# Weight decoding moved partly into the first stage, and filter products in batches of four pairs, in a long-convolution kernel with two MoE layers

## The chip, the cores and the metric

The kernel runs on one core of one Trainium2 chip. The metric is the device time of one execution in microseconds (us). An execution profiled by the hardware gives the trace; the time of that execution stands beside its span.

## The reference, cut to what matters

The sequence has S = 12480 rows of D = 128. First a gated long convolution, then two feed-forward layers with 2048 hidden units:

```python
h_filt = (np.maximum(pos_emb @ w1, 0.0) @ w2) * window        # window = exp(-0.01 * pos)
u = x * v
y = irfft(rfft(u, 2 * S) * rfft(h_filt, 2 * S), 2 * S)[:S]
x = x * y
x = np.maximum(x @ w_in, 0.0) ** 2 @ w_out                    # moe
g = elu(x @ w_in2);  out = g @ w_out2                         # moe2
```

All weights of the two layers reach the kernel as 64-bit floats (each pair of 32-bit words is one number).

## The kernel before, in words

The transform length is L = 181 * 127, and the convolution is done by matrices in three stages. **Stage 1** (`phase1`, lines 179 to 305) folds x * v and the filter's hidden layer and transforms over 181 points: 16 groups of eight channels in a loop over j, each with two calls of `s1` (line 276, 16 matmuls each, line 281), 32 calls in all; the index of the call is i. `prologue(i)` (line 347) hangs other work onto that loop: at i = 15 the loads of the filter's last matrix, of the matrix g and of the first six tables `tb` (line 310); at i = 24 `s2r(0)`; at i = 31 `hmm(0)`. The x tiles of stage 1 live in ten rotating buffers `xc` of the pool `xv`.

**Stage 2** (`phase2`, line 439) goes over NP = 46 pairs of frequencies, p = 0 to 45. Pair p needs on TensorE `s2(p)` (line 461, tile u, the transform of x * v), every second pair `s2r(q)` (line 321, tile rt, the filter's transform of two pairs at once, copied by ScalarE to `rr`) and, one pair later, `hmm(q)` (line 332, tile h: 16 matmuls with 64 rows each, copied by ScalarE to `hh`). VectorE multiplies (`prod`, lines 478 and 479), GpSimd adds and subtracts (lines 481 and 482), TensorE transforms back (`ia`, line 489, tile v, two pairs later), ScalarE copies to z, and SyncE stores z to a buffer in HBM (line 495, and line 500 for the first rows of the last pairs).

Between these, `weights` (line 419) is a generator that decodes and splits the 16 chunks of weights. It is advanced four times per pair; a place, in what follows, is such a step. A chunk's `decode` (line 373) takes four VectorE instructions (lines 380, 382, 391, 393), three of ScalarE (385, 387, 389) and one product on GpSimd (399). Its `split` (line 403) takes a ScalarE copy and a GpSimd subtraction (line 131). A chunk is begun every WDEC = 10 steps, at most WF = 5 are decoded ahead of the splits, and the splits of chunks 0 to 3, 4 to 7 and 8 to 15 wait for pairs 8, 16 and 32 (line 430). Loading (`load_weights`, line 362) runs two chunks ahead in two buffers `raw`.

Each engine works in program order. The order of the work is the order of the calls in the loop at line 554. PSUM has eight banks: in stage 2 two hold u, two v, two h (one buffer, `hbank`) and two rt (two buffers). The pool `p2b` of stage 2 lies where `xv` was, and its first use waits for the last use of `xv`.

**Stage 3** (`phase3`, line 607) runs both layers over 26 tiles of columns. `head` (line 515) prepares its first tile in stage 2.

```python
        while ns < 16 or gs is not None:
            if gd is None and nd < 16 and nd - ns < WF and i >= WDEC * nd:
                gd, nd = self.decode(nd), nd + 1
```

Of the kernel before, what the change touches and what calls it, by code (L numbers as in the profile page):

```python
# [10 lines left out]
F32 = mybir.dt.float32  # L11
F32R = mybir.dt.float32r
U32 = mybir.dt.uint32
AF = mybir.ActivationFunctionType
ALU = mybir.AluOpType
SYNC = mybir.DependencyInfo(mybir.DependencyClass.Sync, mybir.DependencyReason.DATA)
PSUM = bass.MemoryType.PSUM
# [3 lines left out]
D = 128  # L21
# [3 lines left out]
N2 = 127  # L25
# [4 lines left out]
NP = (K1 + 1) // 2  # L30
R = 99
SPLIT = S - (R - 1) * N2
SIZES = (4,) + 24 * (5,) + (3,)
KTAIL = K1 - 64
TBB = 6
WF = 5
AGE = 4
PD = NP - 2
PZ = PD - 4
HD = (33, 35, 36, 37, 38, PZ + 2)  # L40
KD = K1 - 2 * PD
WDEC = 10
OFF = 3
LAG1 = 2
NX = 10
# [75 lines left out]
class Build:  # L121
# [52 lines left out]
        return self.psb[0].tile([128, 2, 512], F32, tag="h", name="h")  # L174

    def rbank(self):
        return self.psb[1].tile([128, 512], F32, tag="rt", name="rt") if len(self.psb) > 1 else self.hbank()[:, 0]

    def phase1(self):
        nc, a = self.nc, self.a  # L180
        with ExitStack() as ctx1:
# [5 lines left out]
            ns = [0]  # L187
# [15 lines left out]
            xvp = self.right.enter_context(self.tc.tile_pool(name="xv", bufs=1, side="right"))  # L203
# [10 lines left out]
            def load_xv(j):  # L214
                for i, (d, nm, n) in enumerate(((xs, "xc", NX), (vs, "vc", NV))):
                    if i and j < 8:
                        t = self.xu[j // 4][:R, 1024 * (j % 4):1024 * (j % 4) + 1024]
                    else:
                        t = xvp.tile([R, 1024], F32, tag=nm, name=nm, bufs=n)
                    d[j] = t.rearrange("p (d h n) -> p d h n", d=8, h=2)  # L220
                    for b, e in ((0, R - 1), (R - 1, R)):
                        nc.sync.dma_start(out=t[b:e], in_=a["xv"][j, i, b:e])
# [47 lines left out]
            def ufold(j):  # L270
                x, v = xs[j], vs.pop(j)
                nc.vector.tensor_tensor(out=v, in0=x, in1=v, op=ALU.mult)
                nc.vector.tensor_tensor(out=x[:, :, 0], in0=v[:, :, 0], in1=v[:, :, 1], op=ALU.add)
                self.sub(nc.vector, x[:, :, 1], v[:, :, 0], v[:, :, 1])
# [19 lines left out]
            for i in range(E // 4):  # L294
                s1(i, [(fold[:, 0, :, 4 * i + c], fold[:, 1, 1:, 4 * i + c]) for c in range(4)], [(self.xr, 2 * K1)], E)
            dst = [(t, n) for t, n in zip(self.xu + [self.xt], (32, 32, 64, 2 * KTAIL))]
            self.raw = {}
            for j in range(D // 8):
                x = xs.pop(j)
                for i in range(2 * j, 2 * j + 2):  # L300
                    s1(i, [(x[:, 4 * (i % 2) + c, 0], x[:, 4 * (i % 2) + c, 1, 1:]) for c in range(4)], dst, D)
                    self.prologue(i)
                if j + NX < D // 8:
                    load_xv(j + NX)
                    ufold(j + NX)

    def buf(self, tag, shape, bufs, dt=F32, pool=None):
        return (pool or self.p2).tile([128] + list(shape), dt, tag=tag, name=tag, bufs=bufs)
# [20 lines left out]
        self.copy(rr, ps[:, :N2 * n])  # L329
        self.st["rr", q] = rr  # L330

    def hmm(self, q):
        rr = self.st.pop(("rr", q))
        ps = self.hbank()
        n = len(self.twin(q))
        for c in range(n):
            for r in range(2):
                e = slice(E * r, E * r + E)
                self.nc.tensor.matmul(ps[:N2, r, D * c:D * c + D], lhsT=rr[e, N2 * c:N2 * c + N2], rhs=self.w2[e],  # L339
                                      start=(c == 0), stop=(c == n - 1))  # L340
        hh = self.buf("hh", [4, 2, D], 2)[:N2]
        self.copy(hh[:, :n].rearrange("p k r d -> p r k d"),
                  ps[:N2, :, :D * n].rearrange("p r (k d) -> p r k d", d=D))
        for i in range(2):
            self.st["h", 2 * q + i] = hh[:, 2 * i:2 * i + 2]

    def prologue(self, i):
        nc, a = self.nc, self.a
        if i == 15:
            self.w2 = self.buf("w2", [D], 1)  # L350
            self.g = self.buf("g", [128], 1)
            for p in range(2):
                nc.sync.dma_start(out=self.w2[E * p:E * p + E], in_=a["w2"])
            nc.sync.dma_start(out=self.g, in_=a["g"])
            for p in range(TBB):
                self.load_tb(p)
        if i == 24:
            self.s2r(0)
        if i == 31:
            self.hmm(0)  # L360

    def load_weights(self, c):
        l, k, q = c // 8, c // 4 % 2, c % 4
        raw = self.buf("raw", [4, D, 2], 2, U32, self.p2b)
        src = self.a[(("moe_w_in", "moe_w_out"), ("moe2_w_in", "moe2_w_out"))[l][k]].bitcast(U32)
        if k == 0:
            src = src[:, 1024 * q:1024 * q + 1024].rearrange("p (b d) -> p b d", d=2 * D)
        else:
            src = src[512 * q:512 * q + 512, :].rearrange("(b p) d -> p b d", p=128)
        self.nc.sync.dma_start(out=raw.rearrange("p a b c -> p a (b c)"), in_=src)  # L370
        self.raw[c] = raw

    def decode(self, c):
        nc = self.nc
        raw = self.raw.pop(c)
        low, high = raw[:, :, :, 0], raw[:, :, :, 1]
        e = self.buf("we", [4, D], 2, U32, self.p2b)
        f = self.buf("wf", [4, D], WF, pool=self.p2b)
        t, s, w, m = e.bitcast(F32), e, f, f.bitcast(U32)
        nc.vector.tensor_scalar(out=m, in0=high, scalar1=0xFFFFF, scalar2=None, op0=ALU.bitwise_and)  # L380
        yield
        nc.vector.tensor_scalar(out=e, in0=high, scalar1=1, scalar2=21,
                                op0=ALU.logical_shift_left, op1=ALU.logical_shift_right)
        yield
        nc.scalar.activation(out=f, in_=m, func=AF.Copy, scale=2.0 ** -20, bias=1.0)
        yield
        nc.scalar.activation(out=t, in_=e, func=AF.Relu, bias=self.ebias[:, 0:1], scale=-1.0)
        yield
        nc.scalar.activation(out=e, in_=t, func=AF.Relu, bias=self.ebias[:, 1:2], scale=-8388608.0)
        yield  # L390
        nc.vector.scalar_tensor_tensor(out=f, in0=low, scalar=2.0 ** -52, in1=f, op0=ALU.mult, op1=ALU.add)
        yield
        nc.vector.scalar_tensor_tensor(out=s, in0=high, scalar=0x80000000, in1=e,
                                       op0=ALU.bitwise_and, op1=ALU.bitwise_or)
        if c + 2 < 16:
            self.load_weights(c + 2)
        yield
        yield
        nc.gpsimd.tensor_tensor(out=w, in0=f, in1=s.bitcast(F32), op=ALU.mult)
        yield  # L400
        self.dec[c] = w
# [15 lines left out]
        yield  # L417

    def weights(self):
        self.w, self.dec = {}, {}  # L420
        nd = ns = 0
        gd = gs = None
        i, age = 0, {}
        while ns < 16 or gs is not None:
            if gd is None and nd < 16 and nd - ns < WF and i >= WDEC * nd:
                gd, nd = self.decode(nd), nd + 1
            for c in self.dec:
                age.setdefault(c, i)
            if (gs is None and ns < 16 and ns in self.dec and i >= age[ns] + AGE
                    and self.pair >= (8, 16, 32, 32)[ns // 4]):  # L430
                gs, ns = self.split(ns), ns + 1
            if gd is not None and next(gd, 0) == 0:
                gd = None
            if gs is not None and next(gs, 0) == 0:
                gs = None
            i += 1
            yield

    def phase2(self):
        nc, a, st = self.nc, self.a, self.st  # L440
        ctx0 = self.ctx
        with ExitStack() as self.ctx:
            psu = self.pool("psu", 2, PSUM)
            psv = self.pool("psv", 2, PSUM)
            self.psb.append(self.pool("psb1", 2, PSUM))
            self.pair = 0
            self.right.close()
            n0 = SIZES[0]
            x0 = self.x0pool.enter_context(self.tc.tile_pool(name="x0", bufs=1, side="right"))
            self.x0 = [x0.tile([128, n0 * (R - 1)], F32R, name=nm) for nm in ("xh0", "xl0")]  # L450
            self.p2b = p2b = self.right.enter_context(self.tc.tile_pool(name="p2b", bufs=1, side="right"))
            for c in range(2):
                self.load_weights(c)
            wgen = self.weights()

# [5 lines left out]
            def s2(p):  # L461
# [6 lines left out]
                st["u", p] = ps  # L468
                if p + TBB < NP:
                    self.load_tb(p + TBB)  # L470

# [37 lines left out]
            n = sum(nrs)  # L509
# [44 lines left out]
            for p in range(NP):  # L554
                self.pair = p
                if p in HD:
                    next(hd)
                if p < PD:
                    s2(p)
                if p:  # L560
                    next(wgen, None)
                prod(p)
                if p % 2 == 0 and p + 2 < NP:
                    self.s2r(p // 2 + 1)
                if p:
                    next(wgen, None)
                if p % 2 == 1 and p + 1 < NP:
                    self.hmm((p + 1) // 2)
                if PD <= p + 1 < NP:
                    s2(p + 1)  # L570
                if p:
                    next(wgen, None)
                if 1 < p <= PD:
                    ia(p - 2)
                if p == PD:
                    ia(p - 1)
                next(wgen, None)
# [312 lines left out]
```

## Time and profile before

| | us |
|---|---|
| median of 3 runs | 1384.85 (1384.46 to 1384.91) |
| time of the profiled execution | 1384.91 |
| its span, first to last instruction | 1383.1 |
| TensorE busy / VectorE / ScalarE / GpSimd | 1368.3 / 1189.3 / 1124.0 / 631.5 |
| mean granted TensorE clock, share of full | 0.998 |

Stage 1 ends near 84 us of the span, stage 2 near 220 us; the rest is stage 3. A view with the name of a line, such as L489, means that line of the kernel. "PE" is TensorE, "PEld" its weight loads, "DVE" VectorE, "ACT" ScalarE, "POOL" GpSimd, "SPq" the queue of SyncE that issues DMAs. A bracket at the end of a row gives the idle time of the engine before it and what ended it.

### The profile page before, as it was taken

How to read it: one execution, taken by the hardware profiler on the slowest of the kernel's cores; microseconds unless marked ns; L12 is line 12 of the kernel's file. 1: busy time of each engine (PE TensorE's matmuls, PEld its weight loads, DVE VectorE, ACT ScalarE, POOL GpSimd, SP SyncE). 2: the span in 40 equal slices, each digit the busy share in tenths (PEclk: the TensorE clock that was granted, in tenths of full speed). 3: DMA queues.
4: the chain of work that ended last, by engine and by line, in shares of the span. 5: the costliest groups of instructions: out<-in, count | busy, mean ns of one | idle time of the engine just before them, and what ended most of it. 6: DMA issues, size and time to landing. Idle time of an engine off the chain costs nothing.

```text
span 1383.1 us, 19231 instructions
## 1 busy us (share of the span) xinstructions
PE 1368.3 (99%) x7236; PEld 1157.4 (84%) x7236; DVE 1189.3 (86%) x1251; ACT 1124.0 (81%) x1476; POOL 631.5 (46%) x348
## 2 busy tenths in 40 slices
PE   9999999999999999999999999999999999999998
PEld 9987767888888888888888888888888888888886
DVE  6759986889898889888988898888988898889887
ACT  6778775888888888888888888888888888888885
POOL 3049993546544444444444444444444444444422
PEclk9999999999999999999999999999999999999999
DMA  8747665100111011101110011101110111000000
GB/s 265 219 141 218 199 217 155 34 23 19 42 42 42 0 42 43 42 0 42 42 42 16 26 42 42 38 5 42 42 43 0 42 42 42 0 29 8 8 8 12
DMA packets 43325, 81.49 MB, mean 59 GB/s; under 512 B 3976, under 2 KB 33043, under 8 KB 43233
## 3 DMA queue, kind: packets, MB, share of 16 engines
q1 hardware_dynamic: 43089, 80.14, 19.1%
q8 instruction: 57, 0.93, 0.3%
q14 instruction: 35, 0.29, 0.1%
q10 hardware_dynamic: 144, 0.13, 0.0%
HBM read 61.90 MB, written 18.32 MB: 58 GB/s over the span
## 4 chain that ended last, share of the span: by engine, by line
PE 92%; DVE 2%; POOL 2%; ACT 1%; DMA 1%; issue 1%; SPq 0%; POOLq 0%; DVEq 0%; ACTq 0%
PE h L157 38%; PE y L157 38%; PE s L281 4%; PE h L592 4%; PE v L489 2%; PE u L466 2%; PE h L339 1%; PE s L247 1%; PE rt L326 1%; POOL m L131 1%; POOL pt L481 1%; POOL pt L482 1%; PE y L712 0%; DMA x<-in_xt_dram 0%; DMA Zd<-z 0%
## 5 line engine op out<-in xcount | busy, mean ns | idle before, releaser
L131 POOL TENSOR_TENSOR lo<-g,hi 128x980 fp32r<-128x980 f32 (+4 forms) x206 | 483.3, 2346 | 644.7 <-DVE tn L811 605.9
L157 PE MATMUL h<-xh,m 128*128 128x490 f32 (+4 forms) x1664 | 433.9, 383 | 1.8 <-ACT xh L134 1.2
L157 PE MATMUL y<-hi,m 128*128 128x490 f32 (+4 forms) x1632 | 427.7, 384 | 2.5 <-DVE xl L131 1.5
L157 PEld LDWEIGHTS h<-xh,m 128*128 128x128 f32 x1664 | 312.3, 189 | 56.6 <-DVE g L823 1.7
L157 PEld LDWEIGHTS y<-hi,m 128*128 128x128 f32 x1632 | 301.9, 189 | 57.3 <-ACT ys L134 4.0
L754 ACT ACTIVATE tn<-h 128x980 f32<-128x980 f32 (+4 forms) x208 | 202.8, 975 | 177.9 <-PE h L157 174.7
L811 DVE SCALAR_TENSOR_TENSOR tn<-ex,tn 128x980 f32<-128x980 f32 (+4 forms) x208 | 241.6, 1162 | 116.3 <-ACT ex L755 114.1
L131 DVE TENSOR_TENSOR lo<-ex,hi 128x980 fp32r<-128x980 f32 (+4 forms) x200 | 250.9, 1254 | 0.0
L823 DVE SCALAR_TENSOR_TENSOR g<-h,r 128x980 f32<-128x980 f32 (+4 forms) x208 | 239.5, 1151 | 11.7 <-ACT r L819 11.5
L157 PE MATMUL h<-xl,m 128*128 128x490 f32 (+4 forms) x832 | 249.3, 380 | 0.0
L157 PE MATMUL y<-lo,m 128*128 128x490 f32 (+4 forms) x816 | 247.5, 384 | 1.7 <-POOL lo L131 1.5
L837 DVE SCALAR_TENSOR_TENSOR ex<-tn,h 128x980 f32<-128x980 f32 (+4 forms) x208 | 238.2, 1145 | 1.4
L830 ACT ACTIVATE hi<-r 128x980 fp32r<-128x980 f32 (+4 forms) x208 | 211.9, 1019 | 0.9
L819 ACT ACTIVATE r<-h 128x980 f32<-128x980 f32 (+4 forms) x208 | 204.3, 982 | 8.1 <-PE h L157 8.0
L134 ACT ACTIVATE hi<-ex 128x980 fp32r<-128x980 f32 (+3 forms) x200 | 206.2, 1031 | 0.0
L755 ACT ACTIVATE ex<-h 128x980 f32<-128x980 f32 (+4 forms) x208 | 201.0, 966 | 0.0
L157 PEld LDWEIGHTS y<-lo,m 128*128 128x128 f32 x816 | 153.2, 189 | 31.5 <-POOL lo L131 3.8
L157 PEld LDWEIGHTS h<-xl,m 128*128 128x128 f32 x832 | 156.4, 189 | 27.0
L481 POOL TENSOR_TENSOR pt<-pt 127x256 f32<-127x256 f32 x43 | 37.4, 869 | 69.5 <-DVE pt L478 69.1
L592 PEld LDWEIGHTS h<-t,v 91*128 91x128 f32 x492 | 58.9, 192 | 2.0 <-DVE v L602 0.3
L592 PE MATMUL h<-t,v 91*128 91x98 f32 (+1 forms) x492 | 58.6, 274 | 0.2 <-DVE v L602 0.2
L602 DVE TENSOR_TENSOR v<-z 91x256 f32<-91x256 f32 (+2 forms) x100 | 55.4, 557 | 0.0
(83 smaller groups left out, 992.8 us busy)
## 6 DMA issues: line engine op xcount, KB each, us to landing
z<-Zd SPq DMA_DIRECT2D x24, 546.0 KB
Zd<-z SPq DMA_DIRECT2D x45, 256.0 KB
t<-in_t_dram SPq DMA_DIRECT2D x24, 351.9 KB
xc<-in_xv_dram SPq DMA_DIRECT2D x16, 392.0 KB
tb<-in_tf_dram SPq DMA_DIRECT2D x46, 127.0 KB
raw<-in_moe_w_in_dram SPq DMA_DIRECT2D x8, 512.0 KB
raw<-in_moe_w_out_dram SPq DMA_DIRECT2D x8, 512.0 KB
m<-in_xv_dram SPq DMA_DIRECT2D x8, 392.0 KB
```

The source lines that it names most:

```text
L131: return eng.tensor_tensor(out=out, in0=a, in1=b, op=ALU.subtract)
L134: self.nc.scalar.activation(out=out, in_=in_, func=AF.Copy)
L157: self.nc.tensor.matmul(outs[b], lhsT=w[:, b, h], rhs=x[b], start=first and i in ((0,) if one else (0, 2)), stop=last and i in ((5,) if on ...
L592: self.nc.tensor.matmul(ps[:, c:c + nr], lhsT=v[:, i, ri, :], rhs=t3[:, i, ri, :nr], start=(first and i == 0 and ri == 0), stop=(i == len( ...
L602: eng.tensor_tensor(out=v[:, b:b + n, ri], in0=z[:, o:o + n, 0, ri], in1=z[:, o:o + n, 1, 1 - ri], op=ops[ri])
L754: nc.scalar.activation(out=e["tn"], in_=e["h"], func=AF.Tanh, scale=0.5)
L755: nc.scalar.activation(out=e["ex"], in_=e["h"], func=AF.Exp)
L811: after = nc.vector.scalar_tensor_tensor(out=pa["em"], in0=pa["ex"], scalar=1.0, in1=pa["tn"], op0=ALU.add, op1=ALU.mult)
L819: nc.scalar.activation(out=f["r"], in_=f["h"], func=AF.Relu)
L823: nc.vector.scalar_tensor_tensor(out=f["g"], in0=f["h"], scalar=0.0, in1=f["r"], op0=ALU.max, op1=ALU.mult)
L830: nc.scalar.activation(out=f["hi"], in_=f["r"], func=AF.Square)
L837: nc.vector.scalar_tensor_tensor(out=pa["g"], in0=pa["em"], scalar=0.0, in1=pa["h"], op0=ALU.min, op1=ALU.max)
```

## The change

Chunks 0 and 1 (`NE = 2`) are loaded in stage 1 at j = 8 and 9 into buffers `xc`, behind the loads of the filter tables, and decoded at j = 9 and 10 by `early`: eight VectorE instructions and none of ScalarE or GpSimd. They come in VectorE's order behind the last fold of stage 1. Stage 2 decodes the other 14 chunks, one every 11 steps, and begins by loading chunks 2 and 3. Six tables `tb` become eight. `s2r(0)` moves to i = 23, `s2r(1)` is added at i = 27, and all later `s2r` come one even pair earlier (s2r(p/2 + 2) at pair p). The products `hmm` of two q come back to back at every fourth pair: the first in `hbank`, which `s2r` now shares, the second in a new pair of banks `h2`; the second's copy comes one pair later. The banks of rt go away. The descriptor scratch goes from its default to 1024 bytes per partition, and the decoded chunks get fixed buffers.

```diff
-TBB = 6
+TBB = 8
-WDEC = 10
+WDEC = 11
+NE = 2
     def rbank(self):
-        return self.psb[1].tile([128, 512], F32, tag="rt", name="rt") if len(self.psb) > 1 else self.hbank()[:, 0]
+        return self.hbank()[:, 0]
+
+    def h2bank(self):
+        return self.psb[1].tile([128, 2, 512], F32, tag="h2", name="h2")
...
+                c = j - 8
+                if 0 <= c < NE:
+                    self.load_weights(c, xvp.tile([128, 1024], F32, tag="xc", name="xc", bufs=NX).bitcast(U32))
+                if 1 <= c <= NE:
+                    self.early(c - 1)
...
-    def hmm(self, q):
+    def hmm(self, q, ps=None):
         rr = self.st.pop(("rr", q))
-        ps = self.hbank()
+        ps = self.hbank() if ps is None else ps
...
+        self.st["hc"] = q, n, ps
+
+    def hcopy(self):
+        q, n, ps = self.st.pop("hc")
+        hh = self.buf("hh", [4, 2, D], 3)[:N2]
...
-        if i == 24:
+        if i == 23:
             self.s2r(0)
+        if i == 27:
+            self.s2r(1)
         if i == 31:
             self.hmm(0)
+            self.hcopy()
...
+    def early(self, c):
+        nc = self.nc
+        raw = self.raw.pop(c)
+        low, high = raw[:, :, :, 0], raw[:, :, :, 1]
+        t = low.bitcast(F32)
+        f = self.decoded(c)
+        m = f.bitcast(U32)
+        nc.vector.tensor_scalar(out=m, in0=high, scalar1=0xFFFFF, scalar2=None, op0=ALU.bitwise_and)
+        nc.vector.tensor_scalar(out=f, in0=m, scalar1=2.0 ** -20, scalar2=1.0, op0=ALU.mult, op1=ALU.add)
+        nc.vector.scalar_tensor_tensor(out=f, in0=low, scalar=2.0 ** -52, in1=f, op0=ALU.mult, op1=ALU.add)
+        nc.vector.tensor_scalar(out=low, in0=high, scalar1=1, scalar2=21,
+                                op0=ALU.logical_shift_left, op1=ALU.logical_shift_right)
+        nc.vector.tensor_scalar(out=t, in0=low, scalar1=896.0, scalar2=0.0, op0=ALU.subtract, op1=ALU.max)
+        nc.vector.tensor_scalar(out=low, in0=t, scalar1=255.0, scalar2=8388608.0, op0=ALU.min, op1=ALU.mult)
+        nc.vector.scalar_tensor_tensor(out=low, in0=high, scalar=0x80000000, in1=low,
+                                       op0=ALU.bitwise_and, op1=ALU.bitwise_or)
+        nc.vector.tensor_tensor(out=f, in0=f, in1=t, op=ALU.mult)
+        self.dec[c] = f
...
-        nd = ns = 0
+        nd, ns = NE, 0
-            if gd is None and nd < 16 and nd - ns < WF and i >= WDEC * nd:
+            if gd is None and nd < 16 and nd - ns < WF and i >= WDEC * (nd - NE):
...
-            self.psb.append(self.pool("psb1", 2, PSUM))
+            self.psb.append(self.pool("psb1", 1, PSUM))
-            for c in range(2):
+            for c in range(NE, NE + 2):
                 self.load_weights(c)
...
-                if p % 2 == 0 and p + 2 < NP:
-                    self.s2r(p // 2 + 1)
+                if p % 2 == 0 and p + 4 < NP:
+                    self.s2r(p // 2 + 2)
-                if p % 2 == 1 and p + 1 < NP:
+                if p % 4 == 1 and p + 1 < NP:
                     self.hmm((p + 1) // 2)
+                    self.hcopy()
+                    self.hmm((p + 3) // 2, self.h2bank())
+                if p % 4 == 2:
+                    self.hcopy()
...
-    nc = bacc.Bacc("TRN2", target_bir_lowering=False, num_devices=1)
+    nc = bacc.Bacc("TRN2", target_bir_lowering=False, num_devices=1, dynamic_dma_scratch_size=1024)
```

## Rows read from the trace of the kernel before

**Rows 1.** Windows: busy time per engine (PE, PEld, DVE, ACT, POOL), clock, DMA share.

```profile
74.00:82.00 8.00, 8.00 (x106) 7.28 (x108) 0.00 (x0) 5.87 (x24) 0.00 (x0) 1.00 0.01 2
83.80:106.00 22.20, 22.20 (x151) 16.77 (x150) 18.95 (x29) 15.96 (x24) 16.78 (x19) 1.00 0.64 200
106.00:148.00 42.00, 41.22 (x262) 29.52 (x261) 40.29 (x54) 33.40 (x55) 40.74 (x41) 1.00 0.70 214
148.00:175.00 27.00, 27.00 (x179) 19.65 (x178) 26.18 (x36) 20.48 (x32) 24.83 (x26) 1.00 0.71 215
175.00:207.00 32.00, 30.23 (x189) 21.25 (x189) 27.28 (x35) 23.40 (x40) 31.17 (x31) 1.00 0.65 209
```

**Rows 2.** Timeline of PE, two pairs of stage 2 and its last batch: start, us.

```profile
112.90 1.03 PE L466 MATMUL u<-m,tb 127*127 127x256 f32 x4
113.85 1.16 PE L339 MATMUL h<-w,rr 64*127 64x128 f32 x16
114.94 1.13 PE L489 MATMUL v<-pt,g 127*128 127x512 f32 x2
115.90 1.03 PE L466 MATMUL u<-m,tb 127*127 127x256 f32 x4
116.77 1.05 PE L326 MATMUL rt<-tb,xr 127*128 127x127 f32 x8
117.66 1.02 PE L489 MATMUL v<-pt,g 127*128 127x512 f32 x2
118.52 1.03 PE L466 MATMUL u<-m,tb 127*127 127x256 f32 x4
...
206.73 0.93 PE L339 MATMUL h<-w,rr 64*127 64x128 f32 x12 [0.28 <-ACT rr L134]
```

**Rows 3.** Waits from 83 to 212 us: total, times, longest.

```profile
PEld v L489 <- POOL pt L482: 2.6, 2, 1.7
PE v L489 <- DVE pt L478: 2.3, 2, 1.5
```

**Rows 4.** Groups of POOL by shape, 175 to 207 us: busy us, mean ns.

```profile
L131 POOL TENSOR_TENSOR m<-wf,m 128x512 fp32r<-128x512 f32 x7 | 9.5, 1363 | 0.0
L481 POOL TENSOR_TENSOR pt<-pt 127x256 f32<-127x256 f32 x10 | 9.0, 900 | 0.1
L482 POOL TENSOR_TENSOR pt<-m 127x256 f32<-127x256 f32 x10 | 8.5, 847 | 0.8
L399 POOL TENSOR_TENSOR wf<-wf,we 128x512 f32<-128x512 f32 x4 | 5.1, 1274 | 0.0
```

**Rows 5.** Chain that ended last, 70 to 84 us: start, us.

```profile
72.86 1.09 PE h L326 x8
73.95 8.79 PE s L281 x112
```

**Rows 6.** Timeline of DVE at the seam of stages 1 and 2.

```profile
71.81 0.69 DVE L131 TENSOR_TENSOR xc<-vc 99x512 f32<-99x512 f32 x1
85.03 0.69 DVE L478 TENSOR_TENSOR pt<-u,hh 127x512 f32<-127x512 f32 x1 [12.53 <-PE u L466]
```

**Rows 7.** Timeline of SP, and of DVE at the first weights.

```profile
67.74 3.23 SPq L312 DMA_DIRECT2D tb<-in_tf_dram  x6
82.78 0.81 SPq L370 DMA_DIRECT2D raw<-in_moe_w_in_dram  x2
86.92 0.69 DVE L380 TENSOR_SCALAR wf<-raw 128x512 uint32<-128x512 uint32 x1 [0.60 <-DMA raw<-in_moe_w_in_dram]
```

**Rows 8.** Tile raw, 80 to 130 us: ns min/median/max, first and last start.

```profile
L380 DVE TENSOR_SCALAR wf<-raw x7: 558/612/990, 86.9 to 127.6; 128x512 uint32<-128x512 uint32 x7
L382 DVE TENSOR_SCALAR we<-raw x7: 415/948/1490, 87.5 to 128.0; 128x512 uint32<-128x512 uint32 x7
L391 DVE SCALAR_TENSOR_TENSOR wf<-raw,wf x6: 723/1044/1796, 89.1 to 124.1; 128x512 f32<-128x512 uint32 x6
L393 DVE SCALAR_TENSOR_TENSOR we<-raw,we x6: 831/1022/1216, 91.0 to 125.2; 128x512 uint32<-128x512 uint32 x6
```

**Rows 9.** Timeline of POOL and DVE near 195 us.

```profile
195.42 1.28 POOL L399 TENSOR_TENSOR wf<-wf,we 128x512 f32<-128x512 f32 x1
195.44 1.80 DVE L391 SCALAR_TENSOR_TENSOR wf<-raw,wf 128x512 f32<-128x512 uint32 x1
```

**Rows 10.** Chain that ended last, the seam of stages 2 and 3.

```profile
211.77 0.61 ACT z L134
...
216.69 3.20 DMA Zd<-z
...
220.96 6.11 DMA x<-in_xt_dram
```

More of the change, by code (lines that the diff above doesn't have):

```diff
@@ L218, in load_xv @@
                     else:
-                        t = xvp.tile([R, 1024], F32, tag=nm, name=nm, bufs=n)
+                        t = xvp.tile([128, 1024], F32, tag=nm, name=nm, bufs=n)[:R]
                     d[j] = t.rearrange("p (d h n) -> p d h n", d=8, h=2)
@@ L296, in phase1 @@
             dst = [(t, n) for t, n in zip(self.xu + [self.xt], (32, 32, 64, 2 * KTAIL))]
-            self.raw = {}
+            self.raw, self.dec = {}, {}
             for j in range(D // 8):
@@ L340, in hmm @@
                                       start=(c == 0), stop=(c == n - 1))
-        hh = self.buf("hh", [4, 2, D], 2)[:N2]
+        self.st["hc"] = q, n, ps
+    def hcopy(self):
+        q, n, ps = self.st.pop("hc")
+        hh = self.buf("hh", [4, 2, D], 3)[:N2]
         self.copy(hh[:, :n].rearrange("p k r d -> p r k d"),
@@ L356, in prologue, with load_weights @@
                 self.load_tb(p)
-        if i == 24:
+        if i == 23:
             self.s2r(0)
+        if i == 27:
+            self.s2r(1)
         if i == 31:
             self.hmm(0)
-    def load_weights(self, c):
+            self.hcopy()
+    def load_weights(self, c, raw=None):
         l, k, q = c // 8, c // 4 % 2, c % 4
-        raw = self.buf("raw", [4, D, 2], 2, U32, self.p2b)
+        if raw is None:
+            raw = self.buf("raw", [4, D, 2], 2, U32, self.p2b)
+        else:
+            raw = raw.rearrange("p (a b c) -> p a b c", a=4, c=2)
         src = self.a[(("moe_w_in", "moe_w_out"), ("moe2_w_in", "moe2_w_out"))[l][k]].bitcast(U32)
@@ L371, in load_weights, with decoded @@
         self.raw[c] = raw
+    def decoded(self, c):
+        i = c % WF
+        return self.buf(f"wf{i}", [4, D], 1, pool=self.p2 if i < NE else self.p2b)
+    def early(self, c):
[16 more added lines that the diff above has]
+        self.dec[c] = f
     def decode(self, c):
@@ L377, in decode @@
         e = self.buf("we", [4, D], 2, U32, self.p2b)
-        f = self.buf("wf", [4, D], WF, pool=self.p2b)
+        f = self.decoded(c)
         t, s, w, m = e.bitcast(F32), e, f, f.bitcast(U32)
@@ L419, in weights @@
     def weights(self):
-        self.w, self.dec = {}, {}
-        nd = ns = 0
+        self.w = {}
+        nd, ns = NE, 0
         gd = gs = None
```

## The prediction

> **What bounds the kernel now.** I read the windows of stage 2 first, then TensorE's timeline in one period, then its waits, then the groups of GpSimd. The change touches only what lies before 220 us. In the windows [rows 1] the reader is to see that TensorE is busy all the time from 83.8 to 106 us and from 148 to 175 us, and idle for 42 - 41.22 = 0.78 us and 32 - 30.23 = 1.77 us in the other two stretches. So stage 2 runs at TensorE's pace, and it loses 2.55 us where another engine is late. The waits tell which one [rows 3]: the transform back (v) waits for GpSimd's and VectorE's products. These engines have little left: in 106 to 148 us VectorE is busy 40.29 of 42 us and GpSimd 40.74; in 175 to 207 us GpSimd 31.17 of 32 [rows 1]. The rule for this change is therefore: what TensorE saves counts only if GpSimd and VectorE lose work too.
>
> **The sum is made against the profiled execution**, 1384.91 us (span 1383.1 and 1.8 around it), 0.06 us above the median of the three runs.
>
> *TensorE, batches.* From start to start [rows 2], u takes 113.85 - 112.90 = 0.95 us ahead of h but 0.87 ahead of rt; h takes 114.94 - 113.85 = 1.09; v takes 0.96 behind h but 0.86 behind rt. So entering the 64-row products costs 0.08 and leaving them 0.10. The batch of 12 matmuls lasts 0.93, that of 16 lasts 1.16, so four more cost 0.23 and sixteen more 0.92: second products that follow directly cost 0.92 instead of 1.09. A merged batch saves 0.08 + 0.10 + 0.17 = 0.35 us. Before there are 22 calls in stage 2 (pairs 1, 3 to 43), after it 11 double ones (1, 5 to 41): 11 x 0.35 = **-3.9**. Two rows rounded by 0.01 make the 0.92 uncertain by 0.16: the ends are 11 x 0.19 = 2.1 and 11 x 0.51 = 5.6.
>
> *TensorE, the moved transform.* One `s2r` goes into stage 1, where one costs 1.09 us of the chain [rows 5], and stage 1 has TensorE without a gap there [rows 1]: **+1.1**. In stage 2 the one of pair 42 is gone: 116.77 to 117.66 is 0.89 [rows 2]: **-0.9**. ScalarE's copies move with them; in 74 to 82 us it is busy 5.87 of 8 us [rows 1], so one copy more hides in its idle time; without that it would add its 0.6 us once.
>
> *Two chunks leave stage 2.* GpSimd loses two products of 1.27 us [rows 4], VectorE eight instructions, at the medians of [rows 8] 2 x (0.61 + 0.95 + 1.04 + 1.02) = 7.2 us, ScalarE six copies. Where the stalls are matters more. Pair 32 is step 125. Before, chunks 12 to 15 are begun at steps 120, 130, 140, 150, so four products fall into 175 to 207 us, as the rows show [rows 4]. After, chunk 12 is begun at step 110, and only 13, 14, 15 fall there: 1.27 us less for an engine that is late by 1.77 there. In 106 to 148 us likewise one chunk less falls. I take half of the 2.55 us as regained, **-1.2**; the ends are 0, if denser work eats it, and -2.5.
>
> *The early decode.* VectorE is idle from 72.5 to 85.03 us [rows 6], and in 74 to 82 us the DMA engines carry 1% and GpSimd nothing [rows 1]. The six tables are issued from 67.74 for 3.23 us [rows 7]; two more and then the two weight loads put the latter near 72 us. A load took from 82.78 to 86.92, 4.1 us, to be used [rows 7], so VectorE can begin near 76. Its price is not in the trace without GpSimd beside it: the shortest of the four kinds are 0.56, 0.42, 0.72, 0.83 [rows 8]; eight at these (five of one tensor at about 0.5, three of two at 0.8) make 4.9 us, two chunks 9.8, to about 86. The first product is ready at 85.03 + 1.1 = 86.1. So it just fits. At the medians, 0.95 and 1.04, a chunk takes 5 x 0.95 + 3 x 1.04 = 7.9 and the end is at 92. I take the shortest, because GpSimd idles until 85.8 and ScalarE shares nothing with it in these rows.
>
> By the Trainium skill, VectorE: DVE Perf Modes, "The perf-mode tier table", float tensor_scalar from SBUF runs at twice the pace of two-tensor operations. The shortest row of line 382, 0.42, agrees and that of line 380, 0.56 for the same shape, does not; if all five took 0.42, the two chunks would take 9.0 instead of 9.8, and the sum would be the same.
>
> *What stands behind it.* The loads of chunks 2 and 3 wait for the last use of the pool `xv`: before, the last `s1` (82.78); now also the last early instruction. If that ends at 86, they land near 90, and the first decode instruction, which stands ahead of pair 1's product in VectorE's order, holds it to 90.6 instead of about 88. TensorE has two u buffers and asks for that product's end only at pair 3 (near 92.6: now 90.6, plus 1.1, plus 0.9 for the second product of the batch). Cost **+0.3**, ends 0 and +2.5. On SyncE's queue the tables behind these loads are needed four pairs later, and cost nothing.
>
> *Unevenness.* Four pairs no longer take equal time on TensorE (about 2.6, 3.9, 2.6, 1.7), so GpSimd, whose products are asked for two pairs later, has some 1.2 us less slack at the narrow place. **+0.5**, ends 0 and +2.
>
> The rest costs nothing: the shared bank of `s2r` is free (`hcopy` has the second product, v and u, 2.9 us, to finish a copy of one), z's second copy has two pairs, and the smaller descriptor scratch has no row: if each issue took SyncE a tenth longer than 0.81 / 2 [rows 7], its waits would hide it, so I take 0, with ends 0 and +0.5 that the range has room for.
>
> At the end of stage 2 the chain goes through ScalarE's z and the stores [rows 10], which follow v; they shift with it, and so does stage 3.
>
> Sum: -3.9 + 1.1 - 0.9 - 1.2 + 0.3 + 0.5 = -4.1 us: 1384.91 - 4.1 = **1380.8 us**, which is 4.05 below the median. All ends together reach from -7.9 to +2.6.
>
> **The rivals.**
>
> *GpSimd binds (1383.6).* For it: its 40.74 of 42 and 31.17 of 32 us [rows 1]. Then merging pays only where it isn't behind, in 83.8 to 106 and 148 to 175 us, 18 of 46 pairs: four batches, -1.4; its removed products give -2.5; the transform +1.1, and in the bound stretch its removal gives nothing; the start +0.3; unevenness 1.2. Together -1.3. Against it: part of its busy time is waiting: lines 481 and 482 take 0.90 and 0.85 on average [rows 4], and it falls with VectorE's decodes. An L391 that began 0.02 us behind a product of GpSimd took 1.80 us [rows 9], against 0.72 at the least [rows 8]. The Trainium skill, SBUF — State Buffer, "SBUF: two separate sides", says that GpSimd and some VectorE operations hold a shared port for a whole instruction and the other one blocks; the trace agrees by that 1.80.
>
> *Everything is regained (1378.3).* Batches -4.3, all stalls -2.5, no cost at the seam: 1.1 - 0.9 - 4.3 - 2.5 = -6.6.
>
> *The early decode is late (1388.3, slower).* Place: VectorE between 76 and the first product. Price: at the longest rows of lines 380, 391 and 393 [rows 8], 5 x 0.99 + 1.80 + 2 x 1.22 = 9.2 us a chunk, two chunks take 18.4, to 94.4; chunks 2 and 3 land at 98.5, and pair 1's product ends 0.6 + 1.3 later, at 100.4, where TensorE wants it at 92.6: +7.8, and with -4.4 for the rest +3.4. It decides once the early decode ends past 94. Against it: GpSimd, beside which those long rows arose, has nothing to do there [rows 1].
>
> *The batch isn't one.* If the second half waits for its copy `rr`, the -3.9 goes: 1384.7. The copy comes from a transform one pair earlier, as before, so this is unlikely.
>
> **How the numbers follow.** Forecast 0.50, GpSimd binds 0.25, everything regained 0.13, early decode late 0.06, no batch 0.06. A measurement tells 0.2%, 2.8 us, from no change. Faster by that: 0.46 of the forecast's 0.50 (its ends reach across), 0.13, and 0.03 of GpSimd's: 0.62. Slower: 0.06 and 0.02 of the ends: 0.08. Same: 0.30. The range, 1377.8 to 1384.8, takes in GpSimd's case and the large gain, and leaves out the late decode and the extreme ends, some 0.15. The forecast's own range is 1378.8 to 1382.8.
>
> **What would show it.** In the trace after: h in 11 groups of 32 matmuls near 2.0 us; stage 1 longer by 1.1; VectorE's eight instructions twice between 76 and 86; the first product near 86; the last v 4 to 5 us earlier; the TensorE idle time in 106 to 207 us below 2.5. The prediction is wrong if that idle time grows to 4 or more with GpSimd named as the releaser, or if the first products of stage 2 start after 88.

## The result and the profile after

The changed kernel takes **1391.56 us** (median of five runs, 1390.4 to 1394.9), the kernel before 1384.71 us beside it (five runs, 1384.41 to 1384.91). The ratio is 1.0051, 95% interval 1.0041 to 1.0062: slower by 6.85 us, where 4.05 us less were forecast. The time is outside the range, and it moved the other way.

The profiled execution took 1390.71 us, 5.80 more than that of before. The page's span and busy time:

```profile
span 1388.9 us, 19222 instructions
PE 1366.8 (98%) x7236; PEld 1154.0 (83%) x7236; DVE 1188.5 (86%) x1259; ACT 1120.5 (81%) x1470; POOL 625.3 (45%) x346
```

From TensorE's timeline the run splits in three. The first u of stage 2 starts at 85.42 us (before 83.80), the last v at 221.99 (before 215.15). So the start is 1.62 later, stage 2 is 136.57 - 131.35 = 5.22 longer, and the rest, 1388.9 - 221.99 = 1166.9 against 1383.1 - 215.15 = 1168.0, is 1.0 shorter. The loss lies in stage 2. Its windows after, cut about as in [rows 1] (columns: stretch and its length, then busy us of PE, PEld, DVE, ACT, POOL, then clock, DMA share, GB/s):

```profile
85.40:108.00 22.60, 20.84 (x144) 15.57 (x143) 17.89 (x29) 14.25 (x22) 13.90 (x16) 1.00 0.58 180
108.00:150.00 42.00, 39.79 (x268) 28.84 (x267) 37.23 (x50) 32.54 (x53) 38.58 (x39) 1.00 0.66 199
150.00:177.00 27.00, 25.08 (x160) 18.12 (x159) 22.87 (x32) 17.17 (x28) 22.27 (x25) 1.00 0.61 184
177.00:213.00 36.00, 32.95 (x206) 23.22 (x205) 26.56 (x37) 25.48 (x43) 32.92 (x35) 1.00 0.63 200
```

TensorE, never idle in two of the four stretches of [rows 1], is now idle in all: 1.76 + 2.21 + 1.92 + 3.05 = 8.94 us, against 2.55. The other engines are less busy than before in the two middle stretches too, so none of them took TensorE's place by mere load; the loss is in waits. The waits of 83 to 222 us (total, times, longest), where before had 2.6 and 2.3 us in two times each [rows 3]:

```profile
PEld v L531 <- POOL pt L524: 9.6, 12, 1.4
ACT wf L427 <- DVE wf L422: 9.0, 6, 3.3
DVE wf L422 <- POOL m L132: 6.0, 3, 3.5
...
PE v L531 <- POOL pt L524: 5.0, 9, 1.0
...
PEld h L335 <- ACT hh L135: 4.6, 4, 2.1
PE h L335 <- ACT hh L135: 3.0, 3, 1.7
...
DVE wf L422 <- DMA raw<-in_moe_w_in_dram: 2.9, 1, 2.9
```

PE and PEld are two records of one wait, so their totals are not added. L422 is the first instruction of a decode; it waits for a load (2.9 us, where before had 0.6 [rows 7]) and for GpSimd (6.0 us, where before had nothing). Both waits can be followed.

**Wait 1, the seam.** VectorE's timeline: the first instruction of the early decode, its last, and what comes behind:

```profile
77.98 0.43 DVE L403 TENSOR_SCALAR wf<-xc 128x512 uint32<-128x512 uint32 x1 [4.02 <-DMA xc<-in_moe_w_in_dram]
...
86.29 0.70 DVE L412 TENSOR_TENSOR wf<-wf,xc 128x512 f32<-128x512 f32 x1
87.13 0.69 DVE L520 TENSOR_TENSOR pt<-u,hh 127x512 f32<-127x512 f32 x1
...
91.30 0.43 DVE L422 TENSOR_SCALAR wf<-raw 128x512 uint32<-128x512 uint32 x1 [2.89 <-DMA raw<-in_moe_w_in_dram]
91.64 0.42 DVE L424 TENSOR_SCALAR we<-raw 128x512 uint32<-128x512 uint32 x1
91.98 0.68 DVE L520 TENSOR_TENSOR pt<-u,hh 127x512 f32<-127x512 f32 x1
```

The early decode ends at 87.0. Only then does SyncE issue the load of chunk 2, and the decode that waits for it holds pair 1's product to 91.98. The chain of waits shows what the forecast had not followed (start, us, what):

```profile
87.07 4.21 DMA raw<-in_moe_w_in_dram
...
91.30 0.44 DVE wf L422
...
91.76 0.63 ACT wf L427
92.39 0.92 ACT hh L135
...
93.36 1.16 PE h L335 x8
```

ScalarE's order also has a decode instruction (line 427) ahead of the copy `hh` of the first filter product. That copy frees the bank that the next `s2r` now shares, and TensorE stands idle for 1.73 us, until 93.36.

**Wait 2, the buffers of decoded weights.** VectorE's timeline, and GpSimd's at the same place:

```profile
110.97 0.67 DVE L521 TENSOR_TENSOR m<-u,hh 127x512 f32<-127x512 f32 x1
115.15 0.43 DVE L422 TENSOR_SCALAR wf<-raw 128x512 uint32<-128x512 uint32 x1 [3.51 <-POOL m L132]
115.49 0.68 DVE L520 TENSOR_TENSOR pt<-u,hh 127x512 f32<-127x512 f32 x1
```

```profile
113.85 1.27 POOL L132 TENSOR_TENSOR m<-wf,m 128x512 fp32r<-128x512 f32 x1
```

Five buffers hold decoded chunks, so chunk 5 needs the buffer of chunk 0, which is free when GpSimd has done the subtraction of chunk 0's split (line 132). That split still begins at step 29 (pair 8 and what GpSimd has queued decide), but chunk 5, begun at step 50 before, is now begun at 11 x (5 - 2) = 33. VectorE waits 3.51 us at its queue's head with pair 9's product behind it.

### The profile page after: what moved, and what is told of

Its sections match the earlier page's. It is cut to its first block, busy times and chain, and to the rows that moved or that the text cites. A ratio compares the mean times of both kernels' runs of the same rounds, so it can differ in the third digit from the quotient of the medians.

```text
span 1388.9 us, 19222 instructions
## 1 busy us (share of the span) xinstructions
PE 1366.8 (98%) x7236; PEld 1154.0 (83%) x7236; DVE 1188.5 (86%) x1259; ACT 1120.5 (81%) x1470; POOL 625.3 (45%) x346
## 4 chain that ended last, share of the span: by engine, by line
PE 82%; DMA 5%; DVE 5%; POOL 4%; ACT 2%; issue 1%; SPq 0%; DVEq 0%; POOLq 0%; ACTq 0%
PE h L158 38%; PE y L158 38%; PE h L638 4%; DMA m<-in_xv_dram 2%; DMA vc<-in_xv_dram 1%; POOL pt L523 1%; POOL m L132 1%; POOL pt L524 1%; POOL wf L441 1%; DMA xr<-in_post_dram 1%; PE v L531 1%; DVE pt L520 1%; DVE ex L883 1%; DVE tn L857 0%; PE u L508 0%
```

## The experiments

Times are medians; ratios, with their 95% intervals, are to the kernel before, timed beside them (its medians were 1384.7 to 1385.1 us). A ratio weighs all runs and is not the quotient of two medians. Edits are against the changed kernel unless said otherwise.

**Which half costs?** Batches alone (no early decode):

```diff
-WDEC = 11
-NE = 2
+WDEC = 10
+NE = 0
```

> The batches of four pairs and the moved transform alone; all 16 chunks are decoded in stage 2, every ten steps, as before. Theory A (the loss is VectorE waiting at the head of its queue, for the load of chunk 2 and for a buffer of decoded weights): neither wait is there, so 1381 to 1383 us, faster than before by 2 to 4. Theory B (the loss is the uneven batches and the bank that the transform now shares with the products): 1388 or more.

The early decode alone, with `hmm`, the banks, the six tables and the places of `s2r` as before:

```diff
-                if p % 4 == 1 and p + 1 < NP:
+                if p % 2 == 1 and p + 1 < NP:
...
-                    self.hcopy()
-                    self.hmm((p + 3) // 2, self.h2bank())
-                if p % 4 == 2:
```

> The early decode and the step of eleven alone; products and transforms as before, with their own banks. Theory A: both waits of VectorE are there, 1387 to 1390. Theory B: 1382 to 1384.5, no loss.

Batches alone took 1388.24 us (1.0023, 1.0013 to 1.0033), the early decode alone 1389.6 (1.0042, 1.0030 to 1.0055). Either half loses by itself, 3.3 and 4.6 us by the medians. The early decode alone has the same two waits:

```profile
DVE wf L417 <- POOL m L132: 6.0, 3, 3.5
...
DVE wf L417 <- DMA raw<-in_moe_w_in_dram: 2.9, 1, 2.9
```

Batches alone have next to nothing of these (0.4 and 0.6 us) and lose in another way. In the profiled run stage 2 begins 3.61 us later: 1.1 is the transform, 0.35 a table that comes late, and TensorE is idle for 1.02 us at 7 us and 0.95 us at 48 us, for a load and a copy far ahead of anything that the change moves; the changed kernel's own profile has neither. Stage 2 is 1.05 us longer where 4.8 less were forecast. The time is the one that theory B gave, but for the shared bank TensorE is idle only 0.5 us in this run; the transform back waits for GpSimd:

```profile
PEld v L531 <- POOL pt L524: 8.0, 9, 2.5
```

**Is wait 1 the order at the seam?** Chunk 2 is begun four places later, behind pair 1's product:

```diff
-            if gd is None and nd < 16 and nd - ns < WF and i >= WDEC * (nd - NE):
+            if gd is None and nd < 16 and nd - ns < WF and i >= max(WDEC * (nd - NE), 4):
```

> The changed kernel, but chunk 2 is begun four steps later, behind pair 1's product instead of ahead of it. Theory A: the first product of pair 1 no longer waits for the load (it began 3.4 us behind its input), 2 to 3 us less than the changed kernel, near 1389. Theory B: no change, 1391 to 1392.

It took 1387.45 us (1.0022, 1.0012 to 1.0032), 4.1 less than the changed kernel and more than theory A gave. VectorE's timeline of this run: pair 1's product no longer stands behind the decode. Wait 2 is shorter in this run too, 3.2 us in three times instead of 6.0, so not all of the 4.1 is wait 1.

```profile
88.39 0.69 DVE L520 TENSOR_TENSOR pt<-u,hh 127x512 f32<-127x512 f32 x1 [0.64 <-PE u L508]
...
90.63 0.43 DVE L422 TENSOR_SCALAR wf<-raw 128x512 uint32<-128x512 uint32 x1 [0.96 <-DMA raw<-in_moe_w_in_dram]
```

**Is wait 2 the number of buffers?** A sixth one:

```diff
-WF = 5
+WF = 6
```

> The changed kernel with six buffers of decoded weights instead of five, and so up to six chunks ahead. Theory A: chunk 5 no longer waits for chunk 0's split (3.5 us at 115 us), 2 to 3 us less than the changed kernel, near 1389. Theory B and a third one, C (GpSimd is the bound): no change, 1391 to 1392.

It took 1389.74 us (1.0037, 1.0024 to 1.0049), 1.8 less, which by itself is within the noise: the intervals overlap. The trace tells more: stage 2 is 133.79 us long instead of 136.57, and the decode that waited 3.51 us follows its predecessor at once:

```profile
113.87 0.67 DVE L521 TENSOR_TENSOR m<-u,hh 127x512 f32<-127x512 f32 x1
114.46 0.57 DVE L422 TENSOR_SCALAR wf<-raw 128x512 uint32<-128x512 uint32 x1
```

The profiled run itself took 1392.53 us, 2.8 above the median, because its stage 1 is 3.7 us longer than the changed kernel's. TensorE was idle 1.98 us ahead of the first transform, for its table, and behind that the granted clock was at its lower level, 1.2 of 2.4 GHz, for part of 4 us (the column behind POOL's, as a share of full, is the mean of each stretch):

```profile
74.00 1.92 PE L335 MATMUL h<-tb,xr 127*128 127x127 f32 x8 [1.98 <-DMA tb<-in_tf_dram]
```

```profile
74.00:76.00 2.00, 2.00 (x10) 1.78 (x12) 1.29 (x2) 0.00 (x0) 0.00 (x0) 0.55 0.98 271
76.00:78.00 2.00, 2.00 (x18) 1.59 (x20) 0.00 (x0) 0.60 (x1) 0.00 (x0) 0.60 0.85 199
```

The transform and the 64 matmuls behind it took 81.81 - 74.00 = 7.81 us, in the changed kernel's profile 78.11 - 71.94 = 6.17. So a table that came 2 us late cost 3.6.

**Does the place of the transforms matter?** Only they are moved, by one call:

```diff
-        if i == 23:
+        if i == 24:
             self.s2r(0)
-        if i == 27:
+        if i == 28:
             self.s2r(1)
```

> The changed kernel with the two transforms of stage 1 at calls 24 and 28 instead of 23 and 27, and nothing else. In one profile the first transform waited 4.1 us for its table in stage 1, in others 1.3 to 1.8. If that wait is what spreads the changed kernel's times (1390.4 to 1394.9) and part of its loss: 1389.5 to 1391 with a spread below 2 us. If not: 1391 to 1392, as wide as before.

A miss: 1392.78 us (1.0053, 1.0041 to 1.0066), no gain. (The waits of 4.1 and of 1.3 to 1.8 us that the expectation names are not in the traces: for the table of the first transform TensorE was idle 1.98 us in the run with six buffers and at most 0.35 in the others.) In the profiled run (1392.96 us) stage 2 starts at 85.18 instead of 85.42, but it is 2.5 us longer than the changed kernel's. Wait 1 is there as before, VectorE 2.8 us for the load, and this time TensorE was idle 2.51 us, not 1.73. Behind that its granted clock fell to the lower level, which it had not done behind the 1.73:

```profile
DVE wf L422 <- DMA raw<-in_moe_w_in_dram: 2.8, 1, 2.8
```

```profile
93.90 1.25 PE L335 MATMUL h<-tb,xr 127*128 127x127 f32 x8 [2.51 <-ACT hh L135]
```

```profile
96.00:98.00 2.00, 2.00 (x6) 1.22 (x5) 0.51 (x1) 1.30 (x2) 1.95 (x2) 0.50 0.11 26
```

The four groups from this transform on took 99.17 - 93.90 = 5.27 us, against 96.94 - 93.36 = 3.58. So the later transforms are not what costs here; a longer wait 1 and the clock behind it are.

**All three together**, with the batches and without:

```diff
-WF = 5
+WF = 6
-        if i == 23:
+        if i == 24:
-        if i == 27:
+        if i == 28:
-            if gd is None and nd < 16 and nd - ns < WF and i >= WDEC * (nd - NE):
+            if gd is None and nd < 16 and nd - ns < WF and i >= max(WDEC * (nd - NE), 4):
```

> The changed kernel with three mends together: chunk 2 begun four steps later, six buffers of decoded weights, and the two transforms of stage 1 at calls 24 and 28 instead of 23 and 27 (behind the tables' landing). If those waits are the whole loss: stage 2 near 129.6 us from the first u to the last v (130.4 before, 135.7 in the changed kernel), stage 1 longer by 1.1, so 1384 to 1385.5. If the batches and GpSimd cost more beside: 1386 or more.

> The early decode alone (no batches, the transform of two pairs where it was), with chunk 2 begun four steps later and six buffers. Theory A: both waits gone, two chunks' work gone from VectorE and GpSimd, so 1382.5 to 1384.5, at or below the kernel before. If the early decode costs by itself (its loads and VectorE's time in stage 1): 1387 or more, near the early decode alone (1389.6).

With the batches 1386.67 us (1.0012, 1.0003 to 1.0021): 4.9 of the 6.85 us are back. (The two lengths in the first expectation are 0.9 us shorter than those used here, from start to start; stage 2 of this run is 132.51.) Without the batches 1385.36 (1.0004, 0.9995 to 1.0013). So the new waits made up most of the loss, but without them the kernel still isn't faster, and the gain on TensorE is missing.

**Where is TensorE's gain?** The rival: GpSimd binds. A split's subtraction on GpSimd is replaced by a copy on ScalarE, in the mended kernel and in the kernel before. This leaves out the subtraction (the low part of the weights is then not the remainder), so the output is another one; GpSimd loses 16 of its instructions.

```diff
-        self.sub(self.nc.gpsimd, wlo, w, whi.bitcast(F32))
+        self.copy(wlo, w)
```

> The kernel with the three mends, and GpSimd's subtraction in the splits of the weights left out (ScalarE copies the value a second time instead), which takes some 22 us of GpSimd's work out of stage 2. Theory C (GpSimd is what eats TensorE's gain): 4 to 6 us less than the mended kernel, and at least 3 less than the kernel before with the same omission. If TensorE's gain isn't there at all: equal to the kernel before with the same omission, within 1 us but for the 1.1 of stage 1.

> The kernel before with GpSimd's subtraction in the splits left out in the same way. TensorE lost 4 us or so in stage 2 to late products, so 1381.5 to 1383.5 under theory C; without GpSimd's part in it 1385.

The mended kernel comes to 1380.18 us (0.9967, 0.9954 to 0.9979), the kernel before to 1381.5 (0.9974, 0.9964 to 0.9984). The first loses 6.5 us by the omission, as theory C had it. But it is only 1.3 us below the kernel before with the same omission, where theory C had at least 3, and the two intervals overlap. The windows over all of stage 2 (same columns), in order the kernel before, before without the subtraction, mended, mended without it:

```profile
83.80:215.15 131.35, 128.80 (x804) 91.85 (x803) 117.83 (x162) 96.60 (x154) 116.63 (x118) 1.00 0.66 206
```

```profile
83.97:212.13 128.16, 128.16 (x804) 91.66 (x803) 107.85 (x162) 103.09 (x170) 92.73 (x102) 1.00 0.68 211
```

```profile
84.98:217.49 132.51, 126.75 (x796) 90.52 (x795) 111.42 (x157) 92.31 (x147) 110.66 (x116) 1.00 0.64 195
```

```profile
85.56:210.60 125.04, 123.74 (x796) 90.47 (x795) 105.34 (x158) 98.44 (x163) 87.88 (x100) 1.00 0.67 206
```

With the load on GpSimd the mended stage 2 is 1.2 us longer than before; without it 3.1 us shorter, and TensorE's busy time falls from 128.16 to 123.74 us. So inside stage 2 most of the saving is there once GpSimd's load is gone, and none with it. (The mended kernel has the early decode beside the batches; that alone takes nothing from TensorE's work.) Of the 4.42 us, TensorE's own idle time takes 1.30; of the 3.1 that are left, the later start of stage 2 takes 1.6 in these profiles. Mended, with all the load, TensorE is idle for 5.76 us. Its named waits:

```profile
PE v L531 <- POOL pt L524: 2.7, 6, 0.8
PE v L531 <- DVE pt L520: 1.7, 2, 1.0
PE h L335 <- ACT hh L135: 0.7, 1, 0.7
```

Where the second line has VectorE, the weight load of the same matmul has GpSimd's L524, whose addition ended 0.05 us ahead of the matmul. From 107 to 149 us GpSimd is busy 40.81 of 42 us, but VectorE 40.42, so this window alone does not tell which of the two binds:

```profile
107.00:149.00 42.00, 40.52 (x274) 29.83 (x273) 40.42 (x52) 32.41 (x53) 40.81 (x41) 1.00 0.69 214
```

**Can it be had with all the work done?** Two reliefs, added to the mended kernel. The first puts free steps behind each split, four for the first eight chunks and one for the others, so that GpSimd's subtractions come further apart (at the end of `split`):

```diff
+        for _ in range(4 if c < 8 else 1):
+            yield
```

> The kernel with the three mends, and the splits of the weights spread out: four steps more between those of chunks 0 to 7, one more between the others. If GpSimd is the bound only where splits follow each other every five steps, the stretches from pair 8 and pair 16 get shorter: stage 2 from 132.7 to 130 us, 1383.5 to 1385. If its total work is the bound: 1386 to 1387, as with the three mends.

The second gives the last product of every odd chunk's decode to VectorE:

```diff
-        nc.gpsimd.tensor_tensor(out=w, in0=f, in1=s.bitcast(F32), op=ALU.mult)
+        (nc.vector if c % 2 else nc.gpsimd).tensor_tensor(out=w, in0=f, in1=s.bitcast(F32), op=ALU.mult)
```

> The kernel with the three mends, and the last product of the odd chunks' decode on VectorE (0.7 us each) instead of GpSimd (1.3 us): seven products less for GpSimd, 9 us. If GpSimd is the bound, stage 2 from 132.7 to 129, 1382.5 to 1384.5. If VectorE, which gets 5 us more, is as close a bound: 1386 to 1388.

Both together:

> Both of the above. If both relieve GpSimd: below either, 1381.5 to 1383.5, faster than the kernel before. If the two overlap: the better of the two.

They took 1383.82 us (0.9993, 0.9983 to 1.0002), 1384.57 (0.9995, 0.9986 to 1.0004) and 1382.72 (0.9985, 0.9976 to 0.9994). Each relief is worth 2 to 3 us of the mended kernel; either alone leaves it level with the kernel before, both together bring it below. Stage 2 falls from 132.51 us to 129.67 with the spread, though GpSimd is as busy as before (111.11 us, 110.66 mended): what binds is how close its work stands. It falls to 129.72 with the moved products, though VectorE gets more to do (114.50 us instead of 111.42): of the two engines it is GpSimd that binds. To see whose merit the last time is, the reliefs were put into the other combinations: the spread alone in the kernel before, then both reliefs in the kernel before (with its five buffers), in the batches without early decode (with six), and in the mended early decode without batches.

> The kernel before with its splits spread out in the same way. TensorE lost some 5 us in stage 2 to waits: if these came from the dense splits, 1383 to 1384, 1 to 2 less than before; if not, 1384.5 to 1385.5.

> The kernel before with GpSimd relieved in the same way and nothing of the change. If the gain of the best version is the relief alone: 1382 to 1383.5. If the change's two parts give it: 1384 to 1385.5.

> The batches with the later transforms of stage 1 and GpSimd relieved in the same way, but no early decode: what the early decode gives. If taking two chunks out of stage 2 counts: 1384 to 1386. If it is only batches and relief: 1382 to 1383.

> The early decode with all mends and GpSimd relieved (spread splits, odd products on VectorE), but no batches: what the batches give in the best version so far (1382.7). If TensorE's saving counts once GpSimd is relieved: 1384 to 1385.5. If not: 1382 to 1383.

The spread in the kernel before took 1384.3 us (0.9994, 0.9985 to 1.0003): nothing that can be told. With both reliefs:

| | no batches | batches |
|---|---|---|
| no early decode | 1385.65 (1.0004, 0.9995 to 1.0013) | 1385.13 (1.0005, 0.9996 to 1.0014) |
| early decode, mended | **1382.49** (0.9981, 0.9973 to 0.9990) | 1382.72 (0.9985, 0.9976 to 0.9994) |

Down a column the early decode is worth 3.2 and 2.4 us (in the left one a sixth buffer and the later begin of chunk 2 come with it). Across a row the batches are worth nothing, 0.5 and -0.2. Relief alone is worth nothing either (top left). The version that beats both kernels is the early decode with its waits taken away, GpSimd relieved, and no batches: 1382.49 us. Its window of stage 2, and below it that of the one with batches:

```profile
83.92:212.64 128.72, 128.30 (x804) 91.66 (x803) 113.86 (x162) 93.43 (x148) 105.58 (x109) 1.00 0.66 202
```

```profile
85.21:213.60 128.39, 125.17 (x796) 90.35 (x795) 116.66 (x165) 92.19 (x147) 104.47 (x109) 1.00 0.67 201
```

In the first TensorE is idle for 0.42 us of 128.72: there it is the bound. With the batches it has 3.13 us less to do and is idle for 3.22, so stage 2 gains 0.33, and it starts 1.29 later, mostly by the transform in stage 1. What TensorE waits for here is no longer GpSimd. Its longest waits with the batches:

```profile
PE v L533 <- DVE pt L526: 1.4, 2, 0.9
PE h L335 <- DMA tb<-in_tf_dram: 0.7, 1, 0.7
PE h L335 <- ACT hh L135: 0.6, 1, 0.6
```

The first is at the end of the stage, where VectorE adds the last pairs; the third is the shared bank. No run took these three away.

## Why the prediction was wrong

Two steps failed. The first is that TensorE's saving and half of the stalls were entered as time; if these terms (3.9, 0.9 and 1.2) are struck out of the sum, 1.1 + 0.3 + 0.5 = 1.9 us more are left, and the mended kernel took 1.7 more than the kernel before. The second is that two waits were priced at 0.3 us or not at all, and taking them away gave 4.9 us. The six terms one by one:

*Batches, -3.9, and pair 42's transform, -0.9.* As TensorE's work both were right in size. A batch shows as forecast, 32 matmuls in 2.04 us:

```profile
110.39 1.03 PE L508 MATMUL u<-m,tb 127*127 127x256 f32 x4
111.35 2.04 PE L348 MATMUL h<-w,rr 64*127 64x128 f32 x32
113.32 1.13 PE L531 MATMUL v<-pt,g 127*128 127x512 f32 x2
```

From start to start it takes 113.32 - 111.35 = 1.97 us, against 2 x 1.09 before [rows 2] and some 0.1 on each side. Over the stage TensorE's busy time falls by 4.42 us without the subtraction (4.8 forecast). **The first step that failed** is to enter this as time. The forecast's own rule was that TensorE's saving counts only if GpSimd and VectorE lose work too; it then added 4.8 us of TensorE's saving beside 2.5 us of products taken from GpSimd and did not ask stretch by stretch which is larger. With GpSimd's load as it is, nothing of the 4.8 arrives; without GpSimd's subtractions stage 2 gets 3.1. (The 0.16 that made the ends of this term is twice what two rows rounded by 0.01 give, 4 x 0.02; that only widens them.)

*Transform in stage 1, +1.1.* Right: the two transforms of the changed kernel stand 1.08 us each in TensorE's timeline, and stage 2 begins 1.62 later. Of the other half microsecond 0.13 is TensorE's idle time ahead of the first transform, for its table, and 0.26 was there by 42 us, ahead of all that the change moves. That the table could be late at all was not in the sum: it cost 3.6 us in the profiled run with six buffers.

*Half the stalls regained, -1.2.* Wrong in sign. Its count is wrong for one of the two stretches that had stalls: from 108 to 150 us GpSimd starts five products of weights and seven subtractions, just as many as from 106 to 148 before. What it lost fell into the first stretch (two products of weights instead of three), where TensorE had no idle time before. And it argued from counts alone, not from what the earlier begin of every chunk runs into. "Decoded chunks get fixed buffers" stood in the change, and the steps at which chunks begin were worked out for the end of the stage, but not for chunk 5 against the split of chunk 0. That is wait 2, **part of the second step that failed**: 3.51 us the longest, 6.0 in three times. The sixth buffer took it away, and stage 2 was 2.8 us shorter.

*The early decode.* Its price was right, its start late. SyncE's timeline:

```profile
69.34 4.04 SPq L321 DMA_DIRECT2D tb<-in_tf_dram  x8
...
73.49 0.85 SPq L389 DMA_DIRECT2D xc<-in_moe_w_in_dram  x2
```

The weights are issued at 73.5 instead of 72, and the decode begins at 77.98 instead of 76. The two chunks then take 86.29 + 0.70 - 77.98 = 9.0 us, against 9.8 forecast, and end at 87.0 against 86. The five instructions of one tensor took 0.42 to 0.44 us, not 0.5, and the three of two tensors 0.69 to 0.71, not 0.8; from start to start most take another 0.03 to 0.10. By the Trainium skill, VectorE: DVE Perf Modes, "The perf-mode tier table", tensor_scalar in fp32 from SBUF runs at twice the pace of tensor_tensor; the trace agrees in direction, 0.43 us against the 0.70 of line 412, 1.6 times for 128x512. That the 9.0 us which the forecast worked out from a row of 0.42 came out exactly is luck: its 0.8 was too long, and the steps between instructions made up for it.

*The seam, +0.3.* **The other part of the second step that failed.** The mechanism was named, the price was not: pair 1's product came at 91.98 instead of 90.6, and the forecast asked who waits on VectorE and TensorE for it, but not who waits on ScalarE. Its sentence "the shared bank of `s2r` is free" rests on 2.9 us that `hcopy` has for its copy; line 427, 3.3 us late, stood ahead of that copy. Taking the decode out of the way gave 4.1 us. Nor is the bank free later on: past 95 us TensorE is idle for it 0.5 to 1.7 us in every profile with batches. The rival *early decode is late* had this kind of loss, but at a decode that ends past 94; it decided already at 87.

*Unevenness, +0.5.* Not measured by itself. It can be in what remains when the batches run beside a relieved GpSimd: 3.22 us of idle TensorE, put down to several releasers, against 0.42 without batches.

Of the rivals, *GpSimd binds* was right that the batches bring nothing beside GpSimd's load, but the 1383.6 that it gave did not come: the kernel without the two new waits took 1386.67. Of the two signs named for a wrong forecast the first came: TensorE's idle time from 106 to 207 us grew to 6.15 us with GpSimd named as the releaser (5.0 us in nine times). The second did not: the first product of stage 2 starts at 87.13.

**What stays open.** The shares of the two waits (4.1 and 1.8 us by themselves, 4.9 with the transforms moved as well) do not add up; with the spread of these runs that may be noise, and the first mend shortened wait 2 too. How much the unevenness of the pairs costs was not measured. The rest behind stage 2 is 1.0 us shorter in the changed kernel, and that is no gain of the change: in the kernel before, behind an idle time of TensorE of 1.22 us, the granted clock fell to its lower level there,

```profile
222.00:224.00 2.00, 2.00 (x8) 2.00 (x7) 0.73 (x1) 1.56 (x2) 0.00 (x0) 0.50 0.81 275
```

and the first six groups of matmuls took 225.28 - 220.41 = 4.87 us; in the changed kernel's profile it stayed at 1.00 behind the same idle time, and they took 230.28 - 226.97 = 3.31. The spread of the changed kernel's times (4.5 us, against 0.5 before) fits loads that land at different times with the clock's fall behind the longer waits, as two profiles show; that this is the whole of the spread is not shown.

## What to carry to other kernels

When work is moved forward, list every resource it then takes earlier (a queue's head, a ring of buffers, a shared bank) and, for each engine, what stands behind the instruction that will wait; a wait on VectorE reached TensorE here by way of ScalarE's order. An engine at 97% of a stretch beside another at 98% can be a second bound: what was saved on the first was worth nothing here until the other got lighter, so take a load off the second engine in an experiment before building the saving on the first. And measure parts of a change apart and together: here one half was good once its waits were gone and GpSimd was relieved, and the other was worth nothing in all five pairs of kernels with all the work done.

## What the hardware showed that was not expected

With GpSimd idle, a VectorE instruction of one tensor took 0.42 to 0.44 us for 128x512, in all five forms of the early decode, on neighbouring words (line 404) as on every second 32-bit word (the other four); beside GpSimd the same masking took 0.56 to 0.99 [rows 8].

A wait of TensorE can cost nearly twice its length. Behind 1.98 and 2.51 us of idle time the granted clock fell to 1.2 GHz, which cost another 1.6 and 1.7 us; behind 1.73 us, at the place of the 2.51, it did not fall. Behind 1.22 us at the start of stage 3 it fell in the kernel before and did not in the changed one, so the length of the wait alone does not settle it.
